# A Nystrom attention and two-layer MoE kernel: the landmark sums of q move from TensorE to VectorE, and the prologue's steps change order

## The chip, the cores and the metric

The kernel runs on one core of one Trainium2 chip. The metric is device time in microseconds of one execution. Three runs of the kernel before gave 676.70, 676.58 and 675.89 us, median 676.58 us.

## What is computed

The reference is Nystrom attention followed by two feed-forward layers:

```python
q_lm = q.reshape(B, H, 32, S // 32, D).mean(axis=3)       # B 4, H 8, S 576, D 64
k_lm = k.reshape(B, H, 32, S // 32, D).mean(axis=3)
A, Bm, C = sm(q, k_lm), sm(q_lm, k_lm), sm(q_lm, k)       # sm: softmax(scale * a @ b.T)
Z = Bm.T / (norm1(Bm) * norminf(Bm) + 1e-6)
for _ in range(6):
    Z = 2 * Z - Z @ Bm @ Z
x = A @ Z @ C @ v                                         # then (2304, 512)
h = x @ w_in;  x = (h * tanh(softplus(h))) @ w_out        # 512 -> 2048 -> 512
h = x @ w2_in; x = layernorm(h * softmax(h)) * g_ln @ w2_out   # 512 -> 1024 -> 512
```

A landmark is the mean of 18 neighbouring tokens; the kernel forms the sum of the 18 and puts the factor into the scale of the exponentials. All weights arrive as 64-bit floats and are turned into pairs of 32-bit words on the chip.

## The kernel before, in words

Attention is handled in eight pieces: batch b (0 to 3) times head group g (0 or 1, four heads each). For a piece, `attn(b, g)` (line 300) defines these steps:

- `prep(nm)` (line 331) forms the landmark sums of q or of k, a 128 x 64 tile `lmq` or `lmk`. For most pieces VectorE does it with one reduction over the raw 128 x 1152 tile (line 341). For the three entries of `EARLY` (line 588), which are q of the pieces (0, 0), (0, 1) and (1, 0), TensorE adds the 18 tokens up instead: 18 products of the raw q with the identity matrix into one PSUM tile (line 337), which ScalarE copies to `lmq` (line 339).
- `a_chain` (line 571): the scores of all q against the landmarks of k (line 442), transposed by VectorE (line 446), and their softmax in 32-wide groups (`soft`, lines 457 to 471), which gives the tiles `AT`, the left operand of the first GEMM.
- `e_chain` (line 545): the 32 x 32 scores of landmarks against landmarks (line 346), their softmax (lines 363 to 377), its two norms (lines 380 to 389) and six Newton steps. A Newton step is four small products per matrix on TensorE (line 298, tile `pows`) and one addition on VectorE (line 495, the last one 498). Lines 499 and 501 lay the result out as `MT`.
- `c_chain` (line 561): the scores of the landmarks of q against all k (line 353), the maximum (line 394), the exponential (line 401), a transpose on TensorE (line 410), and the product with v (line 429).
- `finish_w` (line 506) multiplies the two results (line 508) and ScalarE copies them to `W` (line 511).

The pieces of batch 0 make the **prologue**. Its steps are handed out one by one in the order of the string `PSEQ` (line 627): `q0` is prep of q for g = 0, `e1` the next step of `e_chain` of g = 1, `w0` is finish_w of g = 0, `d` is one step of `decode` (line 137), which turns the 64-bit weights of the first layer into 32-bit ones on GpSimd (line 151), ScalarE (lines 153, 154) and VectorE (lines 163, 172), and `x` starts the piece (1, 0), whose first step is prep of its q. From the handed-out order a scheduler in the framework lays out the row of instructions of each engine, so a row need not stand where `PSEQ` has it. Each engine works its own row in order.

SyncE issues the loads in a fixed order (lines 682 to 699): q and k of batch 0, the first two weight tiles, v, q and k of the piece (1, 0), then seven weight tiles; a second batch of weight tiles follows after the prologue's code (line 751), into the space that q and k of batch 0 held.

When both `W` of a batch exist, `u_step` (line 604) multiplies them with a quarter of `w_in` (line 612), so that attention's output is never formed. The **main part** is 64 pairs of units: `gemm1` (line 634, products in line 623) multiplies `u` by `AT`, `mish` (line 645) is the activation, `gsplit` (line 651) splits the result into a high and a low part, and `gemm2` (line 662, line 671) multiplies by `w_out`. The other pieces of attention and the rest of `decode` are worked in between. A last part does the second layer with its softmax and normalisation.

Of the kernel before, what the change touches and what calls it, by code (L numbers as in the profile page):

```python
# [27 lines left out]
def nystrom_moe_kernel(  # L28
# [105 lines left out]
    def decode(items, cbuf, own=range(NU)):  # L134

        n = len(items)
        cs = {}

        def start(j):
            if j < n:
                items[j] = items[j]()
                t = items[j][0]
                x = t[:, :, 1].bitcast(F32)
                low = t.rearrange("p n w -> p (n w)").bitcast(U8).rearrange("p (n w) -> p n w", w=8)
                if j in own:  # L150
                    G.tensor_scalar(out=x, in0=x, scalar1=2.0 ** -112, scalar2=None, op0=ALU.mult)  # L151
                else:
                    A.activation(out=x, in_=x, func=AF.Copy, scale=2.0 ** -112)
                A.activation(out=t[:, :, 0], in_=low[:, :, 3], func=AF.Copy, scale=2.0 ** -5, bias=-31.0 / 64)

        start(0)
        yield 0
        start(1)
        yield 0
        for j in range(n + 1):  # L160
            if j < n:
                t, o = items[j][:2]
                V.scalar_tensor_tensor(out=t[:, :, 0], in0=t[:, :, 1], scalar=3, in1=t[:, :, 0],  # L163
                                       op0=ALU.logical_shift_left, op1=ALU.bitwise_or)
                yield max(0, j - 1)
            if j:
                items[j - 1][3](cs.pop(j - 1))
            start(j + 2)
            yield j
            if j < n:  # L170
                cs[j] = cbuf() if o is None else None
                V.scalar_tensor_tensor(out=(cs[j] if o is None else o).bitcast(U32), in0=t[:, :, 1], scalar=0x80000000,
                                       in1=t[:, :, 0], op0=ALU.bitwise_and, op1=ALU.bitwise_or)
                items[j][2](cs[j])
                yield j
# [26 lines left out]
    def w1_items():  # L202
        def item(side, m):
            if side == "i":
                s, a = divmod(m, 2)
                n = 2 * NQ
                return words((w_in, w_raw)[a](s)), w_in(s)[:, a * n:(a + 1) * n], lambda c: None, lambda c: None
            return parts(wr["o", m], wop, f"wo{m}", lambda x: wo.update({m: x}))

        return [lambda x=x: item(*x) for x in order1]  # L210
# [89 lines left out]
    def attn(b, g):  # L300
# [5 lines left out]
        def w(shape, tag, name=None):  # L306
            name = name or tag
            if first and (name, g) in home:
                s, o = home[name, g]
                return view(scr[s], o, shape)  # L310
            pool, bufs = (keep, 1) if tag in KEEP else (att, {"st": 2, "lm": 4}.get(tag, 1))
            return pool.tile(shape, F32, tag=tag, name=name, bufs=bufs)

        def ps(k=None):
            if first and k is None:
                bank_n[0] += 1
                return ps_y.tile([P, 512], F32, tag=f"y{bank_n[0] % 4}", name="pa")
            if first and k == "e" and g == 1:
                bank_n[1] += 1
                return ps_h.tile([P, 2, 512], F32, tag="h", name="pa")[:, bank_n[1] % 2]  # L320
            return ps_a.tile([P, 512], F32, tag="a", name="pa")
# [9 lines left out]
        def prep(nm):  # L331
            T[nm] = raw[nm, b, g].rearrange("p (h s) -> p h s", h=2)
            lm[nm] = w([P, 2, L], "lm", "lm" + nm)
            if (nm, b, g) in EARLY:
                pt = ps()[:, 0:2 * L]
# [249 lines left out]
    N9 = RH * L  # L585
    KEEP = ("Ce", "CT", "Aw", "A10")
    QK = 'qk'
    EARLY = (("q", 0, 0), ("q", 0, 1), ("q", 1, 0))
    DT = 10
    OWN = (0, 1, 3, 4, 13)  # L590
    PRE = 0
# [32 lines left out]

    hb, gb, yb = {}, {}, {}
    ps_x = []
    PSEQ = 'q0 k0 e0 a0 a0 c0 e0 q1 k1 e0 c0 e1 a0 e0 a1 c0 d c1 e1 a1 e0 a0 d e1 c1 e0 d e1 c0 c1 e1 e0 e0 a0 d e0 a1 e1 a1 c1 e1 e0 d a1 e1 w0 e1 a0 d d w1 a1 a0 a1 a0 x'
    GLB = 2
    HX = 1
    U = NCH * NF  # L630
# [49 lines left out]
    with ExitStack():  # L680
# [19 lines left out]
        w1 = decode(w1_items(), lambda: att.tile([P, R * D], F32, tag="dc", name="dc", bufs=2)[:, 0:2 * DM], OWN)  # L700
# [29 lines left out]
        for g in range(NG):  # L730
            prep, e, c, t, a = attn(0, g)
            for nm, x in (("q", prep("q")), ("k", prep("k")), ("e", e()), ("c", c()), ("t", t), ("a", a())):
                ch[f"{nm}{g}"] = x
        for nm in PSEQ.split():
            if nm == "d":
# [89 lines left out]
        for u, (s_, i) in enumerate(units):  # L825
            x = segs[s_][0] * CR // R, i // 4
# [238 lines left out]
```

## Time and profile before

| | |
|---|---|
| median of three runs | 676.58 us (675.89 to 676.70) |
| the profiled execution, its own time | 672.18 us |
| its span, first to last instruction | 670.4 us |
| TensorE busy | 639.7 us, 95% of the span |
| VectorE, ScalarE, GpSimd busy | 381.7, 316.0, 41.3 us |
| mean granted TensorE clock | 0.98 of full speed |
| moved by DMA | 55.43 MB, 83 GB/s over the span |

The span is the stretch that the trace covers; the execution's own time is 1.8 us longer. A busy share is an average over all parts. The page also cuts the span into 40 equal slices of 16.8 us each and gives the tenths of each slice in which an engine was busy, and for TensorE the clock that was granted in it; there the parts of the kernel can be told apart.

### The profile page before, as it was taken

How to read it: one execution, taken by the hardware profiler on the slowest of the kernel's cores; microseconds unless marked ns; L12 is line 12 of the kernel's file. 1: busy time of each engine (PE TensorE's matmuls, PEld its weight loads, DVE VectorE, ACT ScalarE, POOL GpSimd, SP SyncE). 2: the span in 40 equal slices, each digit the busy share in tenths (PEclk: the TensorE clock that was granted, in tenths of full speed). 3: DMA queues.
4: the chain of work that ended last, by engine and by line, in shares of the span. 5: the costliest groups of instructions: out<-in, count | busy, mean ns of one | idle time of the engine just before them, and what ended most of it. 6: DMA issues, size and time to landing. Idle time of an engine off the chain costs nothing.

```text
span 670.4 us, 12056 instructions
## 1 busy us (share of the span) xinstructions
PE 639.7 (95%) x4916; PEld 546.9 (82%) x4916; DVE 381.7 (57%) x973; ACT 316.0 (47%) x585; POOL 41.3 (6%) x21
## 2 busy tenths in 40 slices
PE   6977989999999999999997999999999999999997
PEld 5656868799889987899875899997888888888886
DVE  1789889952456334512535712555876666666660
ACT  1369996443446433632735533534533334343331
POOL 2420000000000000000005301230000000000000
PEclk9998799999999999999997999999999999999999
DMA  9998122200312110100026202413101111110001
GB/s 320 394 349 330 36 63 81 81 34 29 107 37 71 37 37 1 37 1 18 19 84 184 88 2 82 144 63 99 48 31 48 48 44 51 33 47 32 16 33 47
DMA packets 30583, 55.43 MB, mean 83 GB/s; under 512 B 3648, under 2 KB 19008, under 8 KB 30528
## 3 DMA queue, kind: packets, MB, share of 16 engines
q1 hardware_dynamic: 25344, 49.36, 21.2%
q10 hardware_dynamic: 5184, 5.31, 2.3%
q8 instruction: 38, 0.62, 0.4%
q14 instruction: 17, 0.14, 0.1%
HBM read 44.63 MB, written 10.03 MB: 82 GB/s over the span
## 4 chain that ended last, share of the span: by engine, by line
PE 85%; DMA 5%; DVE 3%; ACT 3%; POOL 1%; issue 1%; SPq 0%; ACTq 0%; POOLq 0%
PE y L671 28%; PE h L623 28%; PE po L623 15%; PE pa L612 3%; PE pa L337 3%; PE pt L967 2%; PE pa L298 2%; DMA r<-in_moe_w_in_dram 2%; DMA yd<-ye 2%; POOL r L151 1%; PE pa L442 1%; PE pa L353 1%; PE pa L429 1%; DVE r L163 1%; DMA r<-in_moe_w_out_dram 1%
## 5 line engine op out<-in xcount | busy, mean ns | idle before, releaser
L671 PE MATMUL y<-gh,hl 128*128 128x288 f32 x1024 | 163.1, 304 | 6.5 <-ACT ye L677 5.8
L671 PEld LDWEIGHTS y<-gh,hl 128*128 128x128 f32 x1024 | 144.2, 192 | 22.2 <-issue 9.8
L623 PE MATMUL h<-AT,u 128*128 128x288 f32 x768 | 125.4, 308 | 5.3 <-ACT u L615 2.3
L623 PEld LDWEIGHTS h<-AT,u 128*128 128x128 f32 x768 | 109.7, 194 | 15.1 <-ACT u L615 4.8
L658 DVE TENSOR_TENSOR gl<-s,gh 128x288 fp32r<-128x288 f32 x128 | 54.9, 466 | 115.4 <-ACT gh L656 59.4
L623 PE MATMUL h<-hl,yb 128*128 128x512 f32 x432 | 103.5, 394 | 1.3 <-DVE st L936 0.9
L623 PEld LDWEIGHTS h<-hl,yb 128*128 128x128 f32 x432 | 79.7, 188 | 18.0 <-DVE st L936 1.3
L623 PE MATMUL po<-hl,lh 128*128 128x512 f32 x288 | 88.9, 390 | 0.0
L671 PE MATMUL y<-gl,hl 128*128 128x288 f32 x512 | 82.4, 298 | 0.0
L656 ACT ACTIVATE gh<-s 128x288 fp32r<-128x288 f32 x128 | 50.2, 436 | 56.6 <-PE y L671 56.3
L671 PEld LDWEIGHTS y<-gl,hl 128*128 128x128 f32 x512 | 72.6, 189 | 2.6 <-issue 1.3
L648 ACT ACTIVATE s<-h 128x576 f32<-128x576 f32 x64 | 41.6, 650 | 69.8 <-PE h L623 65.8
L623 PEld LDWEIGHTS po<-hl,lh 128*128 128x128 f32 x288 | 53.9, 188 | 11.1
L623 PE MATMUL po<-hl,ll 128*128 128x512 f32 x144 | 56.1, 390 | 0.0
L151 POOL TENSOR_SCALAR r<-r 128x1024 f32<-128x1024 f32 x10 | 31.3, 3134 | 374.7 <-DMA r<-in_moe_w_in_dram 311.3
L943 ACT ACTIVATE e<-s,st 128x1024 f32<-128x1024 f32 x18 | 20.7, 1151 | 30.0 <-DVE st L942 29.8
L937 ACT ACTIVATE e<-h,st 128x1024 f32<-128x1024 f32 x18 | 20.1, 1116 | 31.2 <-DVE st L936 31.2
L935 DVE TENSOR_REDUCE st<-h 128x1 f32<-128x1024 f32 x18 | 22.0, 1223 | 20.3 <-PE h L623 15.2
L127 ACT ACTIVATE yb<-y 128x512 fp32r<-128x512 f32 x18 | 11.3, 632 | 46.6 <-PE h L623 45.7
L623 PEld LDWEIGHTS po<-hl,ll 128*128 128x128 f32 x144 | 27.0, 188 | 5.6
L612 PE MATMUL pa<-w,W 64*32 64x512 f32 x256 | 24.5, 615 | 5.3 <-DVE u L616 3.9
L616 DVE TENSOR_TENSOR u<-pa,u 128x512 fp32r<-128x512 f32 x32 | 21.2, 686 | 14.5 <-ACT u L615 14.2
(174 smaller groups left out, 705.2 us busy)
## 6 DMA issues: line engine op xcount, KB each, us to landing
r<-in_moe_w_in_dram SPq DMA_DIRECT2D x8, 1024.0 KB, 7.0
ro<-in_moe_w_out_dram SPq DMA_DIRECT2D x8, 1024.0 KB, 16.7
yd<-ye ACTq DMA_DIRECT2D x32, 144.0 KB, 1.8
y<-yd SPq DMA_DIRECT2D x18, 256.0 KB, 3.2
out_dram<-ob SPq DMA_DIRECT2D x18, 256.0 KB, 2.0
w<-in_moe_w_in_dram SPq DMA_DIRECT2D x4, 1024.0 KB, 9.4
v<-in_v_dram SPq DMA_DIRECT2D x8, 512.0 KB, 4.1
r<-in_moe_w_out_dram SPq DMA_DIRECT2D x4, 1024.0 KB, 4.8
```

Of the source, the lines that this page charges most:

```text
L151: G.tensor_scalar(out=x, in0=x, scalar1=2.0 ** -112, scalar2=None, op0=ALU.mult)
L337: PE.matmul(pt, lhsT=ident, rhs=T[nm].rearrange("p h (l r) -> p h l r", r=R)[:, :, :, m], start=m == 0, stop=m == R - 1)
L612: mm = PE.matmul(po[g][h * L:(h + 1) * L], lhsT=wb[b][r, g, h * L:(h + 1) * L], rhs=w[r, h], start=True, stop=True)
L616: V.tensor_tensor(out=u[:, 1, g], in0=po[g], in1=f(u[:, 0, g]), op=ALU.subtract))
L623: PE.matmul(o, lhsT=a, rhs=b_, start=i == 0, stop=i == n - 1)
L648: A.activation(out=s, in_=h, func=AF.Mish)
L656: A.activation(out=gh[:, e], in_=s[:, e], func=AF.Copy)
L658: V.tensor_tensor(out=gl[:, e], in0=s[:, e], in1=f(gh[:, e]), op=ALU.subtract)
L671: PE.matmul(yb[s_][d][:, 0:N], lhsT=w_out(s, i + e)[:, d * P:(d + 1) * P], rhs=r[:, e], start=i == i0 and e == k == 0, stop=i + 2 == i1 an ...
L935: V.tensor_reduce(out=st[:, 0:1], in_=h, op=ALU.max, axis=AX.X)
L937: A.activation(out=e, in_=h, func=AF.Exp, bias=st[:, 1:2], accum_out=st[:, 2:3])
L943: A.activation(out=e, in_=s, func=AF.Square, bias=st[:, 4:5], accum_out=st[:, 5:6])
```

## The change

No entry is left in `EARLY`, so all landmark sums take the branch of line 341. The string `PSEQ` has the same steps with some in another place: two `d` and several `c`, `a` and `w` steps move by a few places.

```diff
-    EARLY = (("q", 0, 0), ("q", 0, 1), ("q", 1, 0))
+    EARLY = ()
...
-    PSEQ = 'q0 k0 e0 a0 a0 c0 e0 q1 k1 e0 c0 e1 a0 e0 a1 c0 d c1 e1 a1 e0 a0 d e1 c1 e0 d e1 c0 c1 e1 e0 e0 a0 d e0 a1 e1 a1 c1 e1 e0 d a1 e1 w0 e1 a0 d d w1 a1 a0 a1 a0 x'
+    PSEQ = 'q0 k0 e0 a0 a0 c0 e0 q1 k1 e0 c0 e1 a0 e0 a1 d c0 c1 e1 a1 c0 e0 a0 d e1 c1 e0 d e1 c1 e1 e0 e0 a0 d e0 a1 e1 a1 c1 d e1 e0 a1 e1 w0 e1 w1 d d a0 a1 a0 a1 x a0'
```

What this does to the engines' rows is seen in three places. In the pieces below a row with "-" stands in the kernel before alone, one with "+" in the changed one alone; "x18" means that many in a row.

TensorE, from its first product on (`scr_w_94` and `scr_w_93` are q and k of g = 0, `scr_u_96` is q of g = 1, `lmq` and `lmk` the landmark sums):

```order
-L337 MATMUL pa<-scr_w_94,ident 128x64 x18
-L442 MATMUL pa<-scr_w_94,lmk 32x288
+L353 MATMUL pa<-scr_w_93,lmq 32x288
 L346 MATMUL pa<-lmk,lmq 32x32 x4
-L442 MATMUL pa<-scr_w_94,lmk 32x288 x7
-L353 MATMUL pa<-scr_w_93,lmq 32x288 x8
-L337 MATMUL pa<-scr_u_96,ident 128x64 x18
-L380 MATMUL pa<-X_165,ones_65 128x32
+L442 MATMUL pa<-scr_w_94,lmk 32x288 x8
```

Both series of 18 products are gone, and TensorE's first work is the scores. On VectorE the sums of q and of k of g = 0 now stand first, ahead of the three small instructions of lines 683, 684 and 687 that were first before; the sums of g = 1 follow among the first softmax steps. The third series, q of the piece (1, 0), stood in the row of TensorE among the Newton steps of g = 1 and is gone there too.

VectorE, at the end of the Newton steps of g = 1 (`pows_67` and the `MT` made from it; `w_111` and `r_113` are the first weight tiles, `ro_125` the next):

```order
 L468 STREAM_TRANSPOSE ATr<-Aw 128x288
 L499 STREAM_TRANSPOSE pows_67<-pows_67 128x32
-L457 TENSOR_REDUCE sa<-Aw 128x9
+L341 TENSOR_REDUCE lmq<-q 128x64
 L501 TENSOR_TENSOR MT<-pows_67,mask_63 128x128
 L471 TENSOR_TENSOR AT<-ATr,AT 128x288
 L172 SCALAR_TENSOR_TENSOR w_111<-r_113 128x1024
 L163 SCALAR_TENSOR_TENSOR ro_125<-ro_125 128x1024
+L457 TENSOR_REDUCE sa<-Aw 128x9
```

The sum of q of the piece (1, 0) now stands one row ahead of `MT` of g = 1, in the place that a reduction of the softmax had; that reduction is three rows further back.

ScalarE, at its start (here with the semaphores that a row waits for; `X` and `scr_w_93` are results of exponentials):

```order
-L339 ACT_TABLE_LOAD
-L339 ACTIVATE lmq<-pa 128x64 [waits PE_49]
+L368 ACT_TABLE_LOAD [waits DVE_49]
+L368 ACTIVATE X_146,st<-pa,st 128x32 [waits PE_49]
 L154 ACTIVATE w_111<-w_111 128x1024 [waits DMAHW5_49]
-L368 ACTIVATE X_165,st<-pa,st 128x32 [waits DVE_49,PE_49]
-L154 ACTIVATE r_113<-r_113 128x1024 [waits DMAHW6_49]
 L401 ACTIVATE scr_w_93,st<-pa,st 128x288 [waits DVE_49,PE_49]
```

The first table load waited for nothing before; now it stands behind a wait for VectorE, directly ahead of the first exponential. The three copies of line 339 are gone. In ScalarE's whole row there are 21 table loads where there were 23; the two that are missing stood in the first part of the main stage, between the units' activations. The rows of SyncE and GpSimd keep their order.

## Rows read from the trace of the kernel before

**Rows 1.** The page's 40 slices: TensorE busy, and its granted clock, in tenths.

```profile
PE   6977989999999999999997999999999999999997
...
PEclk9998799999999999999997999999999999999999
```

**Rows 2.** Chain of waits, first 45 us: start, length, and what (pieces by time).

```profile
1.22 4.59 DMA scr_w<-in_q_dram
5.95 7.92 PE pa L337 x36
13.86 0.58 PE pa L442
...
17.61 4.51 PE pa L337 x36
...
33.77 0.40 PE pa L298 x16
34.17 1.13 PE pa L337 x8
...
35.55 1.38 PE pa L337 x10
...
37.17 0.42 PE pa L337 x2
...
37.81 0.23 PE pa L337 x2
...
38.29 1.86 PE pa L337 x14
40.14 0.24 PE pa L298 x8
...
41.41 0.20 DVE MT L501
```

**Rows 3.** Busy time of each engine (instructions) in stretches; then clock, DMA share, GB/s.

```profile
core 0: us, PE busy (x) PEld busy (x) DVE busy (x) ACT busy (x) POOL busy (x), PEclk, DMA share, GB/s
0.00:5.81 5.81, 0.00 (x0) 0.00 (x0) 0.70 (x3) 1.28 (x1) 0.80 (x8) 1.00 0.66 168
5.81:41.60 35.79, 33.67 (x420) 25.63 (x420) 21.56 (x80) 12.76 (x32) 11.62 (x4) 1.00 1.02 396
41.60:97.83 56.23, 46.70 (x355) 37.44 (x356) 52.31 (x95) 50.87 (x74) 3.41 (x1) 0.85 0.48 176
47.44:54.27 6.83, 5.01 (x21) 4.66 (x21) 6.24 (x11) 6.15 (x10) 0.00 (x0) 0.50 1.03 415
64.50:74.74 10.24, 8.88 (x42) 7.58 (x39) 9.27 (x17) 10.18 (x17) 0.00 (x0) 0.50 0.19 61
97.83:134.00 36.17, 36.17 (x410) 27.73 (x416) 32.98 (x70) 22.34 (x43) 0.00 (x0) 1.00 0.24 75
```

**Rows 4.** VectorE's instructions in order of time: start, length, line, tiles.

```profile
7.27 1.35 DVE L341 TENSOR_REDUCE lmk<-scr_w 128x64 f32<-128x1152 f32 x1 [5.18 <-DMA scr_w<-in_k_dram]
...
41.00 0.41 DVE L457 TENSOR_REDUCE sa<-Aw 128x9 f32<-128x288 f32 x1
...
48.20 1.21 DVE L163 SCALAR_TENSOR_TENSOR w<-w 128x1024 uint32<-128x1024 uint32 x1
```

**Rows 5.** GpSimd's and TensorE's instructions in order of time.

```profile
28.30 2.96 POOL L151 TENSOR_SCALAR w<-w 128x1024 f32<-128x1024 f32 x1 [9.75 <-DMA w<-in_moe_w_in_dram]
...
33.12 0.42 PE L298 MATMUL pa<-pows 32*32 32x64 f32 x16 [0.34 <-DVE pows L495]
```

**Rows 6.** ScalarE's table loads.

```profile
0.71 1.28 ACT L339 ACT_TABLE_LOAD   x1 [0.71 <-PEq L1049]
...
70.97 1.28 ACT L368 ACT_TABLE_LOAD   x1
```

**Rows 7.** The products with the identity, first two series: ns least, median, most.

```profile
L337 PE MATMUL pa<-scr_w,ident x36: 404/405/443, 5.9 to 13.5; 128*128 128x64 f32 x36
L337 PE MATMUL pa<-scr_u,ident x36: 300/302/361, 17.5 to 21.8; 128*128 128x64 f32 x36
```

## The prediction
> **What bounds the kernel now.** I read the page's slices first [rows 1]. TensorE is busy at nine tenths or more from the seventh slice (about 100 us) to the end, but for one slice in the middle, where the granted clock dips too, and the last. What is late there is late because TensorE has that much to do, and none of the steps that the change moves lies there. So the change can act in one way only: by the moment at which the dense part begins. In the stretch from 97.83 to 134 us TensorE is busy for all of 36.17 us [rows 3]; work that starts earlier there ends earlier by as much.
>
> Next I read the chain of waits up to the first GEMM [rows 2]. It starts with the load of q, which lands at 1.22 + 4.59 = 5.81 us. Then the first series of products with the identity holds it for 7.92 us, the second series for 4.51, and the third, in five pieces between Newton steps, for 1.13 + 1.38 + 0.42 + 0.23 + 1.86 = 5.02. Together 17.45 of the first 41.6 us are spent on the three sums that the change takes off TensorE. The chain's last piece that I use is `MT` of g = 1, made by VectorE and ending at 41.61; the second `W`, the first `u` and the first GEMM hang on it.
>
> The third view is the engines' busy time by stretch [rows 3]. From 5.81 to 41.60 VectorE works 21.56 of 35.79 us (60%), so it has room for sums. From 41.60 to 97.83 it works 52.31 of 56.23 us (93%) and ScalarE 50.87 (90%), while TensorE works 46.70: that stretch, in which the weights are decoded beside the first units, is bound by VectorE and ScalarE, and it begins when the prologue lets go of it. An earlier end of the prologue therefore moves the whole stretch.
>
> **The change, part by part.**
>
> *First series.* One sum on VectorE takes 1.35 us [rows 4]. The sum of q can run from 5.81 to 7.16; k lands just before 7.27 [rows 4], so its sum then ends at 8.6, and the first scores start at about 8.7 in place of 13.86 [rows 2]: 5.2 us gained. The three small instructions of lines 683 to 687 (0.70 us in all, [rows 3], the three before 5.81) stand behind the sums now and run while TensorE makes the scores; nothing needs them until the softmax has gone some steps.
>
> *Second series.* 4.51 us leave the path. In their place VectorE does the sums of q and k of g = 1, twice 1.35, among the softmax steps of g = 0. From 13.86 to 17.61 TensorE makes the scores, 3.75 us [rows 2], and VectorE has little to do then, so most of the 2.7 us is hidden; without that cover all of it would lie on the path. Bounds 0 and 2.7; I take 1.0, nearer to the lower end because the scores are longer than the sums. Gain 3.5 us.
>
> *Third series.* 5.02 us leave, but the Newton steps were going on beside it. A step that meets no product takes 33.77 - 33.12 = 0.65 us ([rows 5], and the piece at 33.77 in [rows 2]). From 33.77 to 40.38 five steps go by in 6.6 us; at 0.65 each they need 3.25, so 3.4 us are gained, not 5.0. Against that stands the sum of q of the piece (1, 0): it is now in VectorE's row directly ahead of `MT`, 1.35 us, where a reduction of 0.41 [rows 4] was. Net 3.4 - 1.35 + 0.41 = 2.4 us; bounds 0 and 4.1.
>
> *ScalarE's table load.* It took 1.28 us at 0.71, when nobody waited [rows 6]. Now it waits for VectorE and stands directly before the first exponential, on the path. Bounds 0 and 1.28; I take 1.28, as the wait and the exponential that needs the table come from the same step.
>
> The chain thus gives 5.2 + 3.5 + 2.4 - 1.3 = 9.8 us. VectorE sets a limit to it: behind 5.81 it has 21.56 us of work up to `MT` [rows 3], plus 3 x 1.35, plus 0.70, less 0.41, that is 25.9; if it never idled, `MT` would end at 31.7 in place of 41.6, a gain of 9.9. It idled for 40% of that stretch before and will not be without idle time now: I take **9.0 us**.
>
> *The stretch behind the prologue.* Two table loads of 1.28 us fewer on ScalarE [rows 6]: between 0 and 2.6 us. ScalarE idles for 10% of that stretch and VectorE for 7%, so both bind in turn; I take half, 1.3. The reduction of 0.41 us that moved behind `MT` falls into VectorE's full row: -0.4. The three ScalarE copies of line 339 and the steps of `PSEQ` that move by a few places I cost at nothing: they end in the same stretch, on rows with the same work. SyncE's and GpSimd's rows keep their order, so no load moves past another.
>
> *The clock.* The granted clock is 0.50, its lower level of 1.2 GHz, from 47.44 to 54.27 and from 64.50 to 74.74 [rows 3], after stretches in which TensorE had gaps. TensorE works 5.01 and 8.88 us in these two, half of which, 6.9 us, is the most that the low level costs there. If both went away that would be gained; if one more of 10.24 us came, 5.1 would be lost. I take the same as before.
>
> Sum: 9.0 + 1.3 - 0.4 = 9.9 us. The profiled execution took 672.18 us, so the changed one should take 662.3. That execution was 4.4 us shorter than the median of the runs, 676.58; the same 9.9 off the median gives **666.7 us**.
>
> **A rule that speaks against it.** The records of the first series took 405 ns each and those of the second, of the same form, 302 [rows 7]: TensorE was slow when it came from idling, faster after 11 us of dense products. The Trainium skill, page "TensorE: Matmul & The Clock Gate", section "What's actually happening", says that the throttled clock is the default and that activity releases it. By that rule the products that are taken away were what raised the clock in the prologue, and the time would go towards the first rival's. The two rows agree with it; no run here shows a prologue without the products.
>
> **The rivals.**
>
> *Slower: the clock stays low.* TensorE's work from 5.81 to 41.60 shrinks from 33.67 to about 16 us and gets gaps. Were the clock then at 1.2 GHz up to the dense part, the 46.70 us of TensorE work of the next stretch, of which 13.9 already run at half speed (39.8 at full speed), would become 79.5, and that stretch 23 us longer than its 56.2; less the 9.9 gained, 690 us. It decides from 20 us of additional TensorE work at the low level on, since each costs half a us. For it: the two low stretches that there are. Against it: each of them ended while TensorE was still in this stretch, between gaps, and the last 23 us of it ran at the full level. Chance 0.05.
>
> *Only the start is gained.* If VectorE, with five sums and decoding in its row, becomes the chain and its waits add up, the second and third series give nothing: 5.2 - 1.28 - 0.94 = 3.0 us, 673.6 us. For it: VectorE's row is followed in order, and the sum before `MT` shows that a step can stand in the wrong place. Against it: 40% of that stretch was idle. Chance 0.16.
>
> *A weight tile is late.* The DMA engines are busy all through the prologue (share 1.02, [rows 3]) and will not deliver earlier. The third weight tile is taken by GpSimd at 28.30 as it lands, done at 31.26 [rows 5], and VectorE first reads it at 48.20 [rows 4]: 17 us of slack, of which 10 would be used. If a later tile has only half as much slack as needed, 5 us are gained: 671.6. Chance 0.04.
>
> *Nothing comes of it*, because the stretch that VectorE and ScalarE bind absorbs the lead: 676.6 us. The change takes nothing but the two table loads from that stretch, but nothing holds its start except the prologue either. Chance 0.03. The remaining **0.72** are for the forecast.
>
> **How the numbers follow.** The forecast's own range runs from 661 (another 0.9 us at VectorE's limit, 1.3 of table loads, and half of what the clock could return) to 672 (a clock interval more). To leave out no more than 2 in 10 it has to take in the second rival: 660 to 674. A measurement of this kernel can tell about 0.2%, 1.35 us, from no change. Faster by more: 0.72 + 0.16 + 0.04 = 0.92; within: 0.03; slower: 0.05.
>
> **What would show it.** Right: no products of line 337 in the trace, the first scores at about 8.7 us, `MT` of g = 1 near 32.6, the first GEMM 9 to 10 us earlier than before, and that lead still there at 130 us and at the end. Wrong: VectorE idle for more than 3 us between 9 and 32 us (second rival); a granted clock of 0.50 for more than 37 us in the first 90 (first rival); GpSimd or ScalarE waiting for a weight tile behind 40 us (third); the lead of the first GEMM gone at 100 us (fourth).

## The result, and the profile after

Four runs of the changed kernel took 664.43 to 664.88 us, median **664.52 us**; four of the kernel before in the same comparison 675.89 to 677.31, median 676.64. The ratio is 0.9822 (95% interval 0.9805 to 0.9839): 12.1 us or 1.8% faster. The forecast was 666.7 us, range 660 to 674. Of all runs below only three, of *fill_four*, were in a second, slower state of the chip (679.02 to 680.63 us at a granted clock of 0.952 to 0.957); its median leaves them out.

The two profiled executions are only 7.3 us apart (672.18 and 664.88): the one of the kernel before was 4.5 us shorter than its median, the one of the changed kernel 0.4 us longer than its own. What the traces can show is therefore the 7.3 us, where the forecast for this pair was 9.9.

The page's 40 slices after the change, for [rows 1] (TensorE busy, and its granted clock, in tenths):

```profile
PE   5688999999999999999997999999999999999997
...
PEclk9758899999999999999997999999999999999999
```

Slices 2 to 5 of the clock read 7588 where they read 9987 before: TensorE has lost its full clock in the prologue. Behind slice 6 the rows are the same, which fits a gain made before that, as the prediction said; how much was made there is told in us below.

Instructions of all engines in order of time, changed kernel (start, length, engine, line, tiles; in brackets the idle time before and what ended it):

```profile
5.24 1.35 DVE L341 TENSOR_REDUCE lmq<-scr_w 128x64 f32<-128x1152 f32 x1 [5.24 <-DMA scr_w<-in_q_dram]
6.68 1.35 DVE L341 TENSOR_REDUCE lmk<-scr_w 128x64 f32<-128x1152 f32 x1
6.79 1.14 PE L353 MATMUL pa<-scr_w,lmq 64*32 64x288 f32 x2 [6.79 <-DMA scr_w<-in_k_dram]
8.09 0.33 PE L346 MATMUL pa<-lmk,lmq 64*32 64x32 f32 x8 [0.16 <-DVE lmk L341]
...
10.14 1.28 ACT L368 ACT_TABLE_LOAD   x1 [10.14 <-DVE st L364]
11.43 0.29 ACT L368 ACTIVATE X<-pa,st 128x32 f32<-128x32 f32 x1
...
19.32 0.65 PE L429 MATMUL pa<-v,scr_u 128*32 128x64 f32 x32
...
22.11 0.43 PE L429 MATMUL pa<-v,scr_u 128*32 128x64 f32 x16 [0.21 <-ACT scr_u L414]
24.87 0.64 PE L429 MATMUL pa<-v,scr_u 128*32 128x64 f32 x12 [2.33 <-issue]
...
25.95 0.23 DVE L495 TENSOR_TENSOR pows<-pa,pows 128x64 f32<-128x64 f32 x1 [2.05 <-PE pa L298]
...
34.90 1.31 DVE L341 TENSOR_REDUCE lmq<-q 128x64 f32<-128x1152 f32 x1
36.13 0.28 DVE L501 TENSOR_TENSOR MT<-pows,mask 128x128 f32<-128x128 f32 x1
```

and of the kernel before:

```profile
14.18 0.32 PE L346 MATMUL pa<-lmk,lmq 64*32 64x32 f32 x6
15.15 0.19 DVE L363 TENSOR_REDUCE st<-pa 128x1 f32<-128x32 f32 x1 [6.54 <-PE pa L346]
```

After the change TensorE's first products are the scores of line 353 at 6.79, which need the sum of q alone. Those that the first softmax needs (line 346) also wait for the sum of k and start at 8.09, where they started at 14.18 before: 6.1 us earlier. `MT` of g = 1 ends at 36.41 (before 41.6), only 5.2 us earlier. In between there is a new wait: at 22.54 TensorE stops for 2.33 us inside line 429, and "issue" says that no engine and no transfer of the program that the profile shows held it. VectorE stands for 2.05 us behind it.

VectorE's waits from 5.81 to 100 us (us in total, times, longest), before the change:

```profile
DVE st L363 <- PE pa L346: 8.1, 3, 6.5
...
DVE pows L495 <- PE pa L298: 2.9, 6, 1.0
...
DVE pows L498 <- PE pa L298: 0.5, 2, 0.3
```

and after it:

```profile
DVE pows L495 <- PE pa L298: 4.2, 4, 2.0
DVE pows L498 <- PE pa L298: 1.2, 1, 1.2
...
DVE st L363 <- PE pa L346: 0.2, 1, 0.2
```

The wait of the softmax for its scores is gone, 8.1 us (6.5 of them before the first softmax, that of g = 0, at 15.15); the waits in the Newton steps have grown from 3.4 to 5.4. Busy time, granted clock, DMA share and GB/s in stretches, before:

```profile
core 0: us, PE busy (x) PEld busy (x) DVE busy (x) ACT busy (x) POOL busy (x), PEclk, DMA share, GB/s
23.00:41.00 18.00, 16.48 (x288) 10.88 (x288) 13.35 (x60) 8.07 (x20) 5.84 (x2) 1.00 1.02 406
...
5.81:100.00 94.19, 82.54 (x810) 64.60 (x814) 75.28 (x178) 65.78 (x107) 15.04 (x5) 0.91 0.67 255
```

and after:

```profile
23.00:41.00 18.00, 11.95 (x109) 4.39 (x108) 14.07 (x34) 6.25 (x11) 5.85 (x2) 0.51 1.02 407
41.00:100.00 59.00, 53.49 (x462) 43.48 (x463) 54.84 (x108) 55.53 (x85) 3.41 (x1) 0.86 0.50 180
5.81:100.00 94.19, 79.42 (x788) 54.54 (x789) 84.82 (x197) 70.14 (x116) 15.09 (x5) 0.82 0.70 263
```

VectorE is busy for 84.82 of these 94.19 us in place of 75.28. Of the 9.54 us more, 3 x 1.35 = 4.05 are the three sums that it took over; the other 5.5 are work that it did not have to do later. The 241st product of line 671, in the dense part, starts at 135.3 us in place of 141.3: a lead of 6.0. At the first GEMM (line 623) the lead was 4.3 (40.7 for 45.0). A granted clock of 0.82 means 2 x 0.18 x 94.19 = 34 us at the lower level, with 17 before (0.91). This leaves out the start of both: the profile gives 1.00 there, but the products of line 442 take 664 to 686 ns each up to 15.7 us before the change, and in the changed kernel 664 to 684 up to 12.3 us and 402 to 517 from 12.8 on. So both kernels begin with slow products, the one before for some 4 us longer.

### The profile page after: what moved, and what is told of

Read it like the earlier page. It is cut to its first block, busy times and chain, and to the rows that moved or that the text cites. A ratio compares the mean times of both kernels' runs of the same rounds, so it can differ in the third digit from the quotient of the medians.

```text
span 663.1 us, 11837 instructions
## 1 busy us (share of the span) xinstructions
PE 629.6 (95%) x4808; PEld 532.7 (80%) x4808; DVE 386.2 (58%) x976; ACT 313.6 (47%) x580; POOL 40.5 (6%) x21
## 4 chain that ended last, share of the span: by engine, by line
PE 87%; ACT 4%; DMA 3%; DVE 2%; issue 1%; POOL 1%; SPq 0%; ACTq 0%; POOLq 0%
PE y L671 30%; PE h L623 28%; PE po L623 15%; PE pa L612 3%; PE pt L967 2%; PE pa L298 2%; DMA r<-in_moe_w_in_dram 2%; PE pa L442 2%; PE pa L429 1%; PE pa L353 1%; POOL r L151 1%; DMA yd<-ye 1%; DMA scr_w<-in_k_dram 1%; DVE r L163 1%; PE pa L410 1%
## 5 line engine op out<-in xcount | busy, mean ns | idle before, releaser
L623 PEld LDWEIGHTS h<-AT,u 128*128 128x128 f32 x768 | 109.8, 195 | 15.1 <-ACT u L615 4.2
L937 ACT ACTIVATE e<-h,st 128x1024 f32<-128x1024 f32 x18 | 20.1, 1117 | 31.2 <-DVE st L936 31.2
L935 DVE TENSOR_REDUCE st<-h 128x1 f32<-128x1024 f32 x18 | 22.0, 1223 | 20.1 <-PE h L623 15.2
L612 PE MATMUL pa<-w,W 64*32 64x512 f32 x256 | 28.1, 642 | 5.1 <-DVE u L616 4.0
L616 DVE TENSOR_TENSOR u<-pa,u 128x512 fp32r<-128x512 f32 x32 | 21.1, 687 | 13.9 <-ACT u L615 13.5
## 6 DMA issues: line engine op xcount, KB each, us to landing
w<-in_moe_w_in_dram SPq DMA_DIRECT2D x4, 1024.0 KB, 10.5
```

The source lines that it names most:

```text
L612: mm = PE.matmul(po[g][h * L:(h + 1) * L], lhsT=wb[b][r, g, h * L:(h + 1) * L], rhs=w[r, h], start=True, stop=True)
L616: V.tensor_tensor(out=u[:, 1, g], in0=po[g], in1=f(u[:, 0, g]), op=ALU.subtract))
L623: PE.matmul(o, lhsT=a, rhs=b_, start=i == 0, stop=i == n - 1)
L935: V.tensor_reduce(out=st[:, 0:1], in_=h, op=ALU.max, axis=AX.X)
L937: A.activation(out=e, in_=h, func=AF.Exp, bias=st[:, 1:2], accum_out=st[:, 2:3])
```

## Experiments

All were run beside the kernel before, whose median was 676.2 to 676.8 us on each chip. "VectorE" is its busy time from 5.81 to 100 us, "lead" that of the 241st product of line 671 against the kernel before; both, like the start of the first GEMM, are of the one profiled execution. That one can lie far from its median: in *third_on_pe* it took 665.66 us, 6.4 less, and is the shortest of the twelve.

| kernel | sums on TensorE | order | median, us (runs) | ratio, 95% | first GEMM | VectorE | lead |
|---|---|---|---|---|---|---|---|
| before | 3 | old | 676.64 (4) | 1 | 45.0 | 75.28 | 0 |
| before_again | 3 | old | 676.97 (10) | 0.9976 to 1.0022 | 45.0 | 74.48 | 0.7 |
| order_only | 3 | new | 679.66 (10) | 1.0027 to 1.0075 | 55.4 | 67.99 | -8.7 |
| third_on_ve | 1st, 2nd | new | 674.07 (10) | 0.9941 to 0.9978 | 49.9 | 73.03 | -4.7 |
| third_on_pe | 3rd | new | 672.05 (12) | 0.9907 to 0.9953 | 43.9 | 80.69 | 3.9 |
| first_on_pe | 1st | new | 665.83 (4) | 0.9818 to 0.9884 | 45.5 | 81.75 | 4.9 |
| second_on_pe | 2nd | new | 665.83 (5) | 0.9821 to 0.9874 | 42.1 | 83.29 | 4.7 |
| the change | none | new | 664.52 (4) | 0.9805 to 0.9839 | 40.7 | 84.82 | 6.0 |
| change_again | none | new | 663.59 (4) | 0.9781 to 0.9840 | 40.8 | 86.38 | 6.9 |
| sums_only | none | old | 663.75 (4) | 0.9764 to 0.9838 | 37.5 | 88.35 | 10.2 |
| table_early | none | new | 660.15 (6) | 0.9736 to 0.9805 | 37.3 | 89.98 | 10.5 |
| sums_table_early | none | old | 660.04 (4) | 0.9737 to 0.9794 | 37.2 | 89.22 | 9.8 |
| fill_two | none | new | 667.35 (6) | 0.9831 to 0.9902 | 42.6 | 81.23 | 2.5 |
| fill_four | none | new | 669.37 (9) | 0.9866 to 0.9915 | 44.5 | 79.83 | 1.6 |

### Which half of the change

*before_again* is the kernel before without an edit.

> The kernel before, unchanged, once more, for a second trace. The first profiled execution of it took 672.18 us, 4.4 us less than the median of its timed runs. If TensorE's clock is what differs from execution to execution, this one takes 676 us and its mean granted clock is below the 0.981 of the first, with a low stretch more or a longer one in the first 100 us. If the clock has no part in it, the mean clock is 0.98 again whatever the time. Ratio to the kernel before: 1.000 within 0.002.

The expected 676 us did not come, but what came, 670.18 us, has a higher clock than the first profile (0.987 for 0.981), so time and clock moved together as the expectation said they would if the clock is what differs. Its ten runs spread from 670.18 to 678.54 us, and the two shortest have the highest granted clock: 670.18 at 0.987 and 672.14 at 0.982, the other eight 676.7 to 678.5 at 0.969 to 0.975. So one execution says little about 5 us here. What decides the clock from one execution to the next is not shown.

*sums_only*, the sums with the old order, and *order_only*, the reverse:

```diff
 sums_only:  EARLY = ()                                         PSEQ of before
 order_only: EARLY = (("q", 0, 0), ("q", 0, 1), ("q", 1, 0))    PSEQ of the change
```

> EARLY is empty as in the change, PSEQ as before. Theory (the three sums held the chain, VectorE had room): nearly all of the gain, 664 to 667 us, ratio 0.982 to 0.986. Rival (the order of the prologue's steps brings the gain): 671 us or more, ratio above 0.992.

> PSEQ as in the change, EARLY as before, so the three sums stay products on TensorE. Theory (the sums): no change, 675 to 678 us, ratio 0.998 to 1.002. Rival (the order): 669 us or less, ratio below 0.990.

The sums bring the whole gain (12.4 us against the 676.17 of that comparison), a little more than the 664 to 667 us expected. The new order brings none: with the products it costs 3.5 us, which neither expectation had, and with the sums it is neither faster nor slower than the old one (664.52 and 663.59 for 663.75).

### Which series

The third series alone on VectorE, and then each of the three alone on TensorE, all with the new order:

```diff
 third_on_ve:  EARLY = (("q", 0, 0), ("q", 0, 1))
 third_on_pe:  EARLY = (("q", 1, 0),)
 first_on_pe:  EARLY = (("q", 0, 0),)
 second_on_pe: EARLY = (("q", 0, 1),)
```

> The change, but q of the pieces (0, 0) and (0, 1) are summed by products on TensorE again; q of the piece (1, 0), the third series, stays on VectorE ahead of MT. The prediction's terms give the third series 2.4 of 9.9 us: 673 to 675 us. If VectorE's sum ahead of MT costs as much as the products did: 676 to 677 us. If the third series was the main hold: 668 us or less.

> The change, but the third series (q of the piece (1, 0)) stays on TensorE; the first two are made by VectorE. Theory of the terms (the prediction's): the third series is worth 2.4 of the 9.0 us on the chain, so about 667 us, 2 to 3 above the change. Rival from the pair of runs before (order alone 679.7, third series on VectorE 674.1, all three 664.5): the third is worth 5.6 and the first two 9.6, so about 670. Rival 'the clock': the products of the third series keep TensorE's clock at its full level in the second half of the prologue, which pays for them: 664 to 665, with a share of the clock at 0.50 between 23 and 50 us that is under half of the 27 us of the change.

> The change, but the first series (q of the piece (0, 0)) stays on TensorE. With the first two on TensorE the time was 674.1, with none 664.5; so the second series is worth 674.1 less this time, and the first this time less 664.5. By the prediction's terms, 5.2 for the first, 1.28 of table load given back (the copy of the first series brings the table in early) and 3.5 for the second: 664.5 + 5.2 - 1.3 = 668.4. Rival 'the clock pays for the first series' (its dense products raise the clock early and hold it): 665 to 666, with the clock at 0.50 for under 15 us before 55 us. Rival 'the series are worth more together than apart': 670 or more.

> The change, but the second series (q of the piece (0, 1)) stays on TensorE; the first and the third are made by VectorE. With the first alone on TensorE the time was 665.8, with the first two 674.1, with none 663.6 to 664.5. Theory 'each series has a worth of its own': the second is worth 674.1 less 665.8, that is 8, so 672. Rival, the prediction's term: 3.5, so 667.5. Rival 'the two hold each other up' (the second series costs much only where it stands behind the first and behind the scores of g = 0, so that the softmax of g = 0 is done before g = 1 has its scores): alone it costs 1 to 3, 665 to 667, and MT of g = 1 comes at 36 to 38.

The third series is worth 679.66 - 674.07 = 5.6 us beside the other two, and 672.05 - 664.52 = 7.5 alone. In *third_on_ve* the time fell into the range of the prediction's terms (673 to 675) by luck: they gave the series 2.4 us and the new order nothing, and it is 5.6 less some 3. In *third_on_pe* the rival from the pair of runs before it (670) came nearest; the terms (667) and the clock (664 to 665) missed. The 7.5 us stand in the medians alone: the profiled execution of *third_on_pe* is only 0.8 us longer than that of the change, so no trace shows where they lie.

The first and the second cost 1.3 us each when they stand alone on TensorE (2.2 against the change's second median), which is at the edge of what these runs can tell, and 674.07 - 664.52 = 9.6 together. Neither has a price of its own. For the first the terms had said 668.4; 665.83 is the time of the rival "the clock pays", but not by its mechanism, for the clock was at 0.50 for 23.9 us before 55 and not under 15. The theory that would make the second worth 8 fell, and the rival that the two hold each other up foretold both the time (665 to 667) and the place of `MT` (36 to 38; it ended at 37.74). Its reason, that VectorE is done with g = 0 before g = 1 has its scores, explains little. Rows of VectorE, first with both on TensorE (*third_on_ve*; line 363 begins a softmax, of g = 0 and then of g = 1):

```profile
15.18 0.19 DVE L363 TENSOR_REDUCE st<-pa 128x1 f32<-128x32 f32 x1 [6.53 <-PE pa L346]
...
23.59 0.22 DVE L385 TENSOR_REDUCE st<-pa 128x2 f32<-128x64 f32 x1 [1.42 <-PE pa L381]
...
25.89 0.19 DVE L363 TENSOR_REDUCE st<-pa 128x1 f32<-128x32 f32 x1 [1.02 <-PE pa L346]
```

with the first alone (*first_on_pe*):

```profile
8.44 1.35 DVE L341 TENSOR_REDUCE lmq<-scr_u 128x64 f32<-128x1152 f32 x1
14.88 0.19 DVE L363 TENSOR_REDUCE st<-pa 128x1 f32<-128x32 f32 x1 [5.08 <-PE pa L346]
...
19.06 0.18 DVE L363 TENSOR_REDUCE st<-pa 128x1 f32<-128x32 f32 x1
```

and with the second alone (*second_on_pe*):

```profile
17.86 0.23 DVE L385 TENSOR_REDUCE st<-pa 128x2 f32<-128x64 f32 x1 [2.94 <-PE pa L381]
...
20.66 0.17 DVE L363 TENSOR_REDUCE st<-pa 128x1 f32<-128x32 f32 x1
```

The long wait, 6.5 us, stands before the softmax of g = 0 and belongs to the first series; with the first alone VectorE fills 1.35 us of it with the sum of q of g = 1. Behind the second series VectorE waits for the norms of g = 0, whose products stand behind it in TensorE's row (line 381: 2.9 us alone, 1.4 with both), and then 1.0 us for the scores of g = 1 with both, not at all alone. The softmax of g = 1, at 13.48 in the change, comes 5.6 us later with the first, 7.2 with the second and 12.4 with both: there the two nearly add up. `MT` of g = 1 comes 2.8, 1.3 and 9.2 us later. So half or more of a delay of 6 or 7 us is made good between these two places, but only a quarter of one of 12; which engine sets how much can be made good was not taken apart.

### The wait for instructions and the table load

*table_early* is the change with one more exponential, of a 128 x 1 tile, at the head of ScalarE's row, which brings the table in before the scores arrive:

```diff
-        V.tensor_copy(out=ones4, in_=mask4.unsqueeze(2).to_broadcast([P, HG, L]))
+        A.activation(out=warm, in_=pows[0][:, 1, 0:1], func=AF.Exp); V.tensor_copy(out=ones4, in_=mask4.unsqueeze(2).to_broadcast([P, HG, L]))
```

> The change, with one more exponential of a 128x1 tile at the head of ScalarE's row, so that the table is loaded before the scores arrive, as in the kernel before. Theory of the prediction (the load of 1.28 us stands on the path): the first exponential of batch 0 comes 1.2 us earlier, at about 10.2, and the time falls to about 663.2. Rival (VectorE's row or TensorE's scores hold the softmax anyway): the first exponential is earlier, MT of g = 1 is not, and the time is 664.5, no change.

It gained 4.4 us, more than either theory allowed. Instructions of this kernel in order of time:

```profile
10.42 0.29 ACT L368 ACTIVATE X<-pa,st 128x32 f32<-128x32 f32 x1 [8.21 <-DVE st L364]
...
19.57 0.65 PE L429 MATMUL pa<-v,scr_u 128*32 128x64 f32 x32
...
22.36 0.47 PE L429 MATMUL pa<-v,scr_u 128*32 128x64 f32 x17 [0.21 <-ACT scr_u L414]
23.50 0.41 PE L429 MATMUL pa<-v,scr_u 128*32 128x64 f32 x11 [0.67 <-issue]
...
32.75 0.28 DVE L501 TENSOR_TENSOR MT<-pows,mask 128x128 f32<-128x128 f32 x1
```

The first exponential comes 1.0 us earlier (10.42 for 11.43), and nothing is left of that at 19.57 and 22.36: the same products ran at 19.32 and 22.11 in the change, 0.25 us earlier, by as much as q landed earlier there (5.24; here VectorE's first sum starts at 5.50). So the load itself was not what the chain waited for: the rival was right in that. Then the wait is 0.67 us in place of 2.33, and `MT` comes 3.4 us earlier, of which the shorter wait is half. The DMA queue that brings instructions has one 16 KB packet there (its share is that of 16 engines' time: 5.2% of 16 x 1.3 us is 1.08 us). In the change it lies in the stretch from 22.0 to 23.3 us,

```profile
q8 instruction: 1, 0.02, 5.2%
```

and with the early load in that from 21.0 to 22.3:

```profile
q8 instruction: 1, 0.02, 5.3%
```

The packet thus lands a microsecond earlier, while TensorE still has work. The Trainium skill, page "Advanced Engine Details and Errata", section "ISA Cache", says that an engine's instructions are held in lines of 16 KB, 256 instructions each. The trace agrees as to the size. And the wait goes by the count: TensorE stops behind its 218th recorded product in the change, its second profile, *sums_only*, *third_on_pe* and both fillers below (behind the 219th in the two kernels with the early load), whatever product is next; in *fill_two* it is one of line 298:

```profile
24.90 0.31 PE L298 MATMUL pa<-pows 32*32 32x64 f32 x6 [0.79 <-issue]
```

In all eight profiles TensorE goes on 1.2 to 1.5 us after the end of the packet, which starts between 21.1 and 22.8. In the six others, the kernel before among them, TensorE needs this product only at 25.2 us or later, the packet starts between 20.1 and 21.7, and there is no such wait. That this is a wait for instructions is argued from these rows; the profile itself says "issue" only. What sets the moment at which a line is asked for, no run here shows.

To see whether the wait recurs, the change was profiled a second time without an edit (*change_again*), and the early load was put on top of the sums with the old order (*sums_table_early*, the edits of *sums_only* and *table_early* together).

> The change itself once more, to see which parts of its prologue recur. In its first profile TensorE waited 2.33 us for its next instruction at 22.54 us, the clock fell to 0.50 at 23.04, and the first GEMM came at 40.72; the kernel with the sums alone waited 0.76 us at that place, and its first GEMM came at 37.5. Theory 'the wait for instructions belongs to this order of rows': it recurs with 2 us or more, the first GEMM comes at 40 to 41 and the median is 664 to 665. Rival 'it was an accident of one execution': the wait is under 1 us, the first GEMM comes at 37 to 38.5, and the profiled execution takes 661 to 662.

> The sums on VectorE with the order of steps of the kernel before, and the extra exponential that loads the table early. Theory 'the table load is on the path': the sums alone gave 663.75, less 1.2 is about 662.5, and the first GEMM comes 1.2 us earlier than their 37.5. Rival 'the early load gained nothing itself': the kernel with the change and the early load had its first exponential 1.0 us earlier and its second group's exponential 1.0 us later (15.49 for 14.52), and won 3.4 us at the first GEMM because the wait for instructions shrank from 2.33 to 0.67 us; the sums alone have that short wait already, so 663 to 664, with the first GEMM at 37.3 to 37.7.

The wait recurred with the same 2.33 us, and the first GEMM at 40.8: it belongs to this kernel's rows and is no accident of one execution. With the old order it is short (0.76 us in *sums_only*), and there the first GEMM comes 3.2 us earlier; the medians of the two orders do not differ. On top of *sums_only* the early load moved the first GEMM by 0.3 us, about what the second theory had said; but the median, 660.04, is 3.7 us lower, which neither had. The profiled executions differ by 1.5 us only (661.17 and 659.72). The rest lies in runs that left no trace; their mean granted clock is 0.975, that of *sums_only* 0.970. What the early load does to the clock of those runs stays open. Both kernels with the early load beat the change: 660.0 and 660.2 us.

### The clock

*fill_two* (shown) and *fill_four* keep TensorE at work: behind each Newton block but the last of the prologue two or four more products with the identity, whose results nobody reads.

```diff
-                pz = ps()[:, 0:2 * L].rearrange("p (a l) -> p a l", a=2)
+                pf = ps(); pz = pf[:, 0:2 * L].rearrange("p (a l) -> p a l", a=2)
                 if i < 6:
-                    blocks(pz, old[:, 0], old)
+                    blocks(pz, old[:, 0], old); [PE.matmul(pf[:, 2 * P:2 * P + 64], lhsT=ident, rhs=ident[:, 0:64], start=True, stop=True) for _ in range(2 if first else 0)]
```

> The change, and two more products with the identity (128x64) behind each of the Newton blocks of batch 0; nobody reads their results, they only keep TensorE at work between the steps. Theory 'the low clock costs': in the change the granted clock is 0.50 from 23.0 to 50.4 us, and MT of g = 1 comes 5 us earlier instead of 9; with the fillers the low stretch is under 15 us, MT comes at 34 or earlier, and the time is 661 to 663. Rival 'the chain does not hang on the clock': the low stretch shrinks, and the time stays at 664 to 665, since VectorE's steps bound the chain. Rival 'the level is not decided by this work': the low stretch stays at 25 to 30 us, and the time is 665 to 667 by the fillers' own 0.1 to 0.4 us each.

> As the one with two, with four such products behind each block (about 0.4 us a block at the full level, 0.8 at the low one). 'The low clock costs': the low stretch shrinks further, under 10 us, and the time is 660 to 663. 'The chain does not hang on the clock': 665 to 667, as the fillers now stand in the way of the other group's step. 'The level is not decided by this work': 667 to 669, as twice the fillers run at the low level.

Both got slower, by 2.8 and 4.9 us. The stretch from 23 to 41 us, first *fill_two*, then *fill_four*, for that of the change above:

```profile
23.00:41.00 18.00, 16.77 (x168) 9.61 (x155) 13.10 (x37) 5.46 (x10) 5.72 (x2) 0.61 1.01 402
```

```profile
23.00:41.00 18.00, 16.68 (x206) 12.09 (x194) 11.17 (x37) 5.68 (x10) 6.30 (x2) 0.85 1.02 405
```

The four products held the clock at 0.85 in place of 0.51, so the level does follow what TensorE does; and VectorE got through less, 11.17 us of work for 14.07. The two products did not shorten the long low stretch: 27.3 us, as in the change; with four it is 20.5. In *fill_two* the wait of line 495 for its products is

```profile
DVE pows L495 <- PE pa L494: 5.8, 10, 0.9
```

Line 494 is that of the added products. They stand in the way of the step that they should speed up. So the theory that the low clock costs was not put to its test, for which the low stretch had to fall under 15 and under 10 us, and the price of the low level was not isolated. That being busy is not all that sets the level is seen in *third_on_pe*, where TensorE is busy for 16.93 us of the same 18, about as long as with four fillers, at 0.60.

## Why the prediction was right, and where its steps failed

**What bounds.** Right for the profiled pair: from the 241st product of line 671 to the end both kernels take the same time but for 1.3 us (529.1 and 527.8 of the span). One sentence was too simple: that an earlier end of the prologue moves the whole stretch behind it. *first_on_pe* has its first GEMM at 45.5, later than the kernel before, and still a lead of 4.9 us. VectorE's account is a better measure of how far a kernel has got. In the table, VectorE's busy time less the 75.28 of before, less 1.35 for each sum that it took over, gives -7.3, -3.6, 2.7, 3.8, 5.3, 5.5, 7.1, 9.0, 10.7, 9.9, 1.9 and 0.5 us for the kernels from *order_only* to *fill_four*; the leads are -8.7, -4.7, 3.9, 4.9, 4.7, 6.0, 6.9, 10.2, 10.5, 9.8, 2.5 and 1.6. All lie within 1.5 us. But this does not show that VectorE is what bounds the first 100 us. It is busy for 91% of the stretch behind 97.83 [rows 3], so a kernel that is some us further at 100 shows nearly as many us more of VectorE's work, whatever brought it there. From 41 to 100 us of the changed kernel ScalarE is as busy as VectorE (55.53 and 54.84 of 59 us). No run gave VectorE or ScalarE alone more work in this stretch, so which of them binds was not tested.

**First series, 5.2 us.** The place was right (the scores of the first softmax at 8.09 for the forecast 8.7; q landed at 5.24 here), though scores of line 353, for which the sum of q is enough, came before it, which the prediction did not see. The size was not: alone it is worth 1.3 to 2.2.

**Second series, 3.5 us.** Alone 1.3 to 2.2, with the first 9.6 together. This step failed in its form: the two were added up as if each had a path of its own, while half or more of either alone is made good before `MT`, and of the two together only a quarter.

**Third series, 2.4 us.** Mis-sized: 5.6 to 7.5. The sum in front of `MT` did take its 1.31 us there, as foreseen.

**Table load, 1.28 us on the path.** It stood between VectorE's result and the exponential (10.14 to 11.43), but nothing of it was left 8 us later: the products of line 429 ran no earlier without it. Yet bringing it forward took 4.4 and 3.7 us off the medians, with a shorter wait in the one case and the first GEMM 0.3 us earlier in the other; where the rest of this gain comes from stays open.

**Order of the steps, costed at nothing.** This holds for the time only where the sums are on VectorE (old order 663.75, new 664.52 and 663.59; with the early load 660.04 and 660.15), though the new order then makes TensorE wait 2.33 us in place of 0.76 and has its first GEMM 3.2 us later. With the products it fails: the new order costs 3.0 to 3.5 us.

**MT near 32.6, with VectorE's limit at 31.7.** It came at 36.4, and the first GEMM 4.3 us earlier and not 9 to 10. The wait behind the 218th product accounts for 2.05 us on VectorE and the wait of line 498 for products at the lower clock for 1.2; *table_early*, where most of the former is missing, had it at 33.03, near the forecast.

**The stretch behind, +1.3 - 0.4.** The lead grew from 4.3 us at the first GEMM to 6.0 at the 241st product of line 671, so the sign was right; that the two table loads did it is not shown.

**The clock, same as before.** Wrong: 34 us at the lower level up to 100 us in place of 17, start of the kernel left out. TensorE works for 27.0 us in these, with 13.9 before, so the first rival's condition, 20 us more, was not met, nor its sign of more than 37 us. What the 13.1 us more cost, at most half of them, was not isolated. The Trainium skill's rule that activity releases the throttle ("TensorE: Matmul & The Clock Gate", "What's actually happening") agrees with this pair of traces: without the products TensorE is busy for 11.95 of the 18 us from 23 to 41 at 0.51, with them for 16.48 at 1.00. Busy time alone does not tell the level, though: *fill_two* has 16.77 us at 0.61.

**Signs of the rivals.** VectorE idled for 3.7 us from 9 to 32 us (19.27 of 23 busy), which by the prediction is the sign of *Only the start is gained*; its time, 673.6 us, did not come. The sign was set too low: *first_on_pe* and *second_on_pe*, with longer waits, still gained 10 us or more.

The total, 9.9 forecast and 12.1 measured, thus came out near in part by luck, since single terms missed by 3 to 5 us either way. Put on after the new order, the sums are worth 679.66 - 664.52 = 15.1 us and the order costs some 3; put on first, they are worth 12.4 and the order nothing. By either way the sums were worth more than 9.9. And of the 12.1 the pair of profiles shows only 7.3; the rest lies in runs without a trace.

## What to carry to other kernels

Do not take the lead at one instruction for the gain: *first_on_pe* was behind at its first GEMM and 4.9 us ahead 90 us later. How much work the busiest engine has done by a fixed time follows the lead (here within 1.5 us in twelve profiles), but it tells how far the kernel has got and not what held it. Two waits behind one another need not be worth the sum of each alone, here 1.3 each and 9.6 together, so take them away singly and together. A change of order can put an engine's wait for its instructions on the path: look for "issue" in the chain. And profile more than once where the runs of a kernel spread by as much as its gain.

## What the runs showed of the hardware

TensorE waited 2.33 us in the middle of a series of products, most likely for instructions, twice to the hundredth, and 0.34 to 0.87 us at the same count of products, 218 or 219, in kernels that differ by a few rows; a 16 KB packet of the instruction queue took 1.08 us beside a DMA share of 1.02, and TensorE went on 1.2 to 1.5 us behind its end. Executions of one and the same kernel spread by 8 us (670.18 to 678.54), and the shorter ones had the higher granted clock: 0.982 and 0.987 against 0.969 to 0.975.
